# A written-out order of 1,500 steps is replaced by another one, and TensorE's matrix products of zeros are taken out

## The chip, the core and the metric

The kernel runs on one core of a Trainium2 chip. The core has a matrix engine (TensorE, PE in the profile), a vector engine (VectorE, DVE), a scalar engine (ScalarE, ACT), a general engine (GpSimd, POOL) and a sequencer that only issues DMAs (SyncE, SP); PEld is TensorE's loading of weights, which overlaps its products. Each engine takes its own instructions strictly in the order in which the program gives them, and waits on semaphores for the others. Sixteen DMA engines move data for all of them. The metric is the time of the kernel on the device in microseconds (us).

## What is computed

The reference is a linear attention whose output goes through a gated long convolution. B is 8, heads 8, S 576, head size 64, features 128, model width 512.

```python
def phi(x):                                   # q and k, with one w_phi [64, 128]
    proj = x @ w_phi
    proj = proj - max(abs(proj), axis=-1)
    return concat([exp(proj), exp(-proj)])    # 256 features
kv  = k_p^T @ v ;  z = sum(k_p)               # per batch and head
att = (q_p @ kv) / (q_p @ z + 1e-6)
x   = att as [B, S, 512]
x1, x2, x3 = split(x @ w_proj, 3)             # w_proj [512, 1536]
x2c = irfft(rfft(x2) * rfft(filter))          # circular convolution over S = 576
out = (x1 * x2c * x3) @ w_out
```

## The kernel before

All data of a batch stay in SBUF; matrix products are in bf16. The work is cut into small methods of one class, and the whole program is one string, `PLAN`: a list of some 1,500 words, each a method with its arguments and, after `@`, the first of the PSUM banks (eight) that it uses. `run()` (line 958) goes through the string and calls the methods:

```python
for word in PLAN.split():
    name, _, bank = word.partition("@")
    self.bank = int(bank) if bank else None
    f, *args = name.split(",")
    getattr(self, f)(*[int(a) if a.isdigit() else a for a in args])
```

So the string fixes the order of instructions on each engine, the engine of those steps that name one (DVE, ACT or POOL), and the banks. Nothing else sets the order: words of different engines stand in one list, but only words of the same engine are ordered by it, and the framework adds the semaphores for data, buffers and banks. `RING` (line 20) says how many buffers a name has.

What the words are, by stage (b is the batch, v a quarter of its rows, X a half):

- **Loads.** `loadh` (L540, halves, batch 0 only) and `load` (L534) bring q, k or v from HBM and cast them to bf16; POOL issues them. `w_load` brings w_phi (SP, L498) and a third of w_proj or w_out (POOL, L502, L505). `filt_load` (SP, L424) brings the filter in 18 pieces.
- **Transposes.** Batch 0 is transposed on TensorE: `T` (L570) and its eviction `Te`. Later batches go through DMA transposes issued by SP: `trh` (L550) for half of q or k, `trm` (L685) for the maxima of q, `trx` (L770) and `trxt` (L775) for the attention's output, `gen_fwd` (L402) and `gen_fwd5` (L407) once for the Fourier matrices.
- **Features.** `Pk` and `Qn` (L589, L596; `Pkt`, `Qnt` L603 for the last ninth of the rows) project k and q; `maxk`, `maxq` (DVE, L656) take the absolute maximum; `ex`, `exkt`, `exqt` (ACT, L640 to L650) the exponentials. `mhi` and `mlo` split the maxima of q into two bf16 parts, `trm` transposes them, and `Pq`, `Pqt` (L617, L623) project q once more, transposed, with the maxima subtracted inside TensorE. So the first `Pq` of a batch needs `trm` to have landed.
- **Attention.** `em` (ACT) and `vs` (POOL, L696) scale v with the maxima of k, `KV` (L711) makes kv and z, `NE`, `NEt` (L732, L741) the numerator and denominator, `rc`, `xn`, `xnt` (DVE) divide.
- **Gate.** `X1`, `X3` (L846) and `X2` (L803, L807) are the three projections; `fold` and `foldt` build sums and differences of x for `X2`. `F` (L444, L460) is the forward Fourier transform, `m1`, `m2`, `m3` the product with the filter's transform (which `H`, `H_ev` make once from `filt_fold`), `I` the inverse transform, `Ie`, `Ip`, `Im` put its halves together, `tm` multiplies x1 by x3, `ym` the result by the convolution, `O` (L938) is the last projection, with `Oa` and `Ob` as its first three quarters and its last in the last batch, `Oe` its eviction and `st` (SP, L954) the store.
- **Zeros.** `warm,n,k` (L300) issues n matrix products of a tile of zeros, 128 x 128k, whose result nobody reads. There are 20 such words with 58 products.
- **Tables.** `gen_rows` to `gen_sin` build the Fourier matrices by sines on ACT, `gen_sel`, `gen_selx` a selection matrix on POOL. [...]

Of the kernel before, what the change touches and what calls it, by code (L numbers as in the profile page):

```python
# [1010 lines left out]
```

## Time and profile before

| | |
|---|---|
| median of 4 runs | 320.96 us (319.53 to 325.91) |
| the profiled execution | 321.4 us, of which its span is 319.6 |
| busy: PE, DVE, ACT, POOL | 284.8, 247.6, 232.2, 222.6 us |
| mean granted clock of TensorE | 0.96 |
| moved by DMA | 41.52 MB |
| products of zeros (L300) | 58, busy for 13.22 us |

The page gives the busy time of each engine, then the span in 40 slices of 8 us with the busy share of each in tenths, the clock that TensorE was granted (9 is 90% or more), and the mean busy share of the DMA engines. Further views give the busy time by stage, the groups of instructions by line, who waited for whom, the chain of work that ended last, and the instructions of one engine in order of time. A busy share of TensorE is modelled and is not TensorE at its peak.

### The profile page before, as it was taken

The numbers are of one execution on the slowest core, as the hardware profiler recorded it, in microseconds if no ns is written. First come the engines' busy times: TensorE is split into PE (matmuls) and PEld (weight loads), VectorE is DVE, ScalarE is ACT, GpSimd is POOL, SyncE is SP. The second block draws the span as 40 slices with busy tenths as digits, with TensorE's granted clock in tenths as the row PEclk, the third lists the DMA queues.
The fourth block names the chain that finished last, engine by engine and source line by source line (L and its number), as shares of the span: only waits on it lengthen the run. The fifth ranks groups of instructions, "written<-read, shape, count | busy, mean of one in ns | idle before, by whom it ended". The sixth has DMA issues, their size and how long they took to land.

```text
span 319.6 us, 9475 instructions
## 1 busy us (share of the span) xinstructions
PE 284.8 (89%) x3915; PEld 163.9 (51%) x3959; DVE 247.6 (77%) x409; ACT 232.2 (73%) x366; POOL 222.6 (70%) x174
## 2 busy tenths in 40 slices
PE   6666597999868999999999999999999999999981
PEld 2344373565554556555656654664475555654430
DVE  4698589799656997889879887898779777767850
ACT  5697586989647778988788777887787787434531
POOL 8859933779854888779679698847879668813230
PEclk9687589999989999999999999999999999999999
DMA  6999999999999998667994546367953223331416
GB/s 116 238 193 171 180 186 171 141 203 166 166 111 169 178 169 154 135 116 112 148 208 105 131 109 113 19 115 140 160 124 75 63 69 53 75 83 34 98 40 159
DMA packets 78667, 41.52 MB, mean 130 GB/s; under 512 B 58976, under 2 KB 73440, under 8 KB 78624
## 3 DMA queue, kind: packets, MB, share of 16 engines
q1 hardware_dynamic: 63808, 24.66, 42.8%
q0 software_dynamic: 14816, 16.25, 36.2%
q8 instruction: 31, 0.51, 0.7%
q14 instruction: 12, 0.10, 0.1%
HBM read 33.75 MB, written 9.44 MB: 135 GB/s over the span
## 4 chain that ended last, share of the span: by engine, by line
PE 76%; DMA 12%; POOL 4%; DVE 3%; issue 3%; ACT 2%; SPq 0%; POOLq 0%; DVEq 0%; ACTq 0%
PE ps L846 17%; PE ps L938 9%; PE ps L803 8%; PE ps L897 8%; DMA mT<-mh 6%; PE ps L460 6%; PE ps L711 6%; PE ps L732 5%; PE ps L617 2%; PE ps L589 2%; PE ps L623 2%; DMA qn<-in_q_dram 2%; DMA xTt<-xnt 2%; PE ps L596 2%; PE ps L853 2%
## 5 line engine op out<-in xcount | busy, mean ns | idle before, releaser
L846 PE MATMUL ps<-xT,wproj 128*128 128x512 bf16 x244 | 62.8, 380 | 0.5
L915 POOL TENSOR_TENSOR yT<-cv,x1s 128x576 bf16<-128x576 f32 x27 | 34.7, 1290 | 30.6 <-DVE cv L905 18.9
L656 DVE TENSOR_REDUCE mq<-ps 128x8 f32<-128x1024 f32 (+1 forms) x40 | 44.1, 1114 | 14.6 <-PE ps L596 12.0
L656 DVE TENSOR_REDUCE mk<-ps 128x8 f32<-128x1024 f32 (+1 forms) x40 | 44.4, 1113 | 6.5 <-PE ps L589 4.1
L696 POOL TENSOR_TENSOR vm<-vn,vm 128x1152 bf16<-128x1152 bf16 x16 | 34.5, 2154 | 11.8 <-ACT vm L690 9.8
L640 ACT ACTIVATE Eqm<-ps 128x1024 bf16<-128x1024 f32 x32 | 32.9, 1028 | 10.0 <-PE ps L623 6.1
L696 POOL TENSOR_TENSOR vp<-vn,vp 128x1152 bf16<-128x1152 bf16 x16 | 34.4, 2149 | 7.8 <-ACT vp L690 5.8
L834 POOL TENSOR_TENSOR t<-C,B 128x1024 bf16<-128x1024 bf16 x15 | 31.8, 2125 | 10.3 <-ACT C L716 9.3
L938 PE MATMUL ps<-wout,yT 128*128 128x512 bf16 x133 | 34.8, 379 | 1.3 <-DVE yT L915 0.8
L640 ACT ACTIVATE Ekm<-ps 128x1024 bf16<-128x1024 f32 x32 | 32.5, 1028 | 4.7 <-PE ps L589 4.1
L897 PE MATMUL ps<-inv,Y 128*128 128x288 bf16 (+1 forms) x192 | 35.6, 289 | 0.1
L640 ACT ACTIVATE Eqp<-ps 128x1024 bf16<-128x1024 f32 x32 | 32.5, 1023 | 3.9 <-PE ps L623 3.8
L640 ACT ACTIVATE Ekp<-ps 128x1024 bf16<-128x1024 f32 x32 | 32.6, 1030 | 3.7 <-DVE mk L656 2.4
L846 PEld LDWEIGHTS <-wproj 128*128 128x128 bf16 x256 | 23.0, 98 | 23.5 <-issue 0.2
L803 PE MATMUL ps<-wproj,eo 128*128 128x512 bf16 x119 | 30.5, 381 | 1.5 <-issue 1.1
L905 DVE TENSOR_TENSOR cv<-es,ps 128x288 f32<-128x288 f32 x64 | 26.2, 448 | 7.2 <-PE ps L897 4.0
L829 DVE TENSOR_TENSOR Y<-ps,A 128x1024 bf16<-128x1024 f32 (+1 forms) x24 | 24.8, 1044 | 6.9 <-PE ps L460 3.0
L839 POOL TENSOR_TENSOR Y<-Y,t 128x1024 bf16<-128x1024 bf16 x12 | 25.5, 2123 | 5.6 <-DVE Y L839 3.5
L716 ACT COPY o<-ps 128x512 f32<-128x512 f32 x27 | 15.8, 587 | 13.6 <-PE ps L938 10.8
L883 DVE TENSOR_TENSOR x1s<-ps,x1s 128x512 bf16<-128x512 f32 x32 | 21.8, 686 | 4.4 <-PE ps L846 3.9
L716 ACT CAST x1s<-ps 128x512 bf16<-128x512 f32 (+1 forms) x34 | 18.7, 553 | 7.0 <-PE ps L846 4.0
L716 ACT CAST x2n<-ps 128x512 bf16<-128x512 f32 (+1 forms) x32 | 16.2, 520 | 10.3 <-PE ps L803 6.8
(149 smaller groups left out, 636.5 us busy)
## 6 DMA issues: line engine op xcount, KB each, us to landing
out_dram<-o SPq DMA_DIRECT2D x72, 128.0 KB, 2.4
vn<-in_v_dram POOLq DMA_DIRECT2D x8, 576.0 KB, 7.8
kn<-in_k_dram POOLq DMA_DIRECT2D x7, 576.0 KB, 9.0
qn<-in_q_dram POOLq DMA_DIRECT2D x7, 576.0 KB, 8.2
wproj<-in_moe_w_proj_dram POOLq DMA_DIRECT2D x3, 512.0 KB, 8.1
fl<-in_moe_filter_fft_dram SPq DMA_DIRECT2D x18, 64.0 KB, 5.1
kn<-in_k_dram POOLq DMA_DIRECT2D x2, 288.0 KB, 5.5
qn<-in_q_dram POOLq DMA_DIRECT2D x2, 288.0 KB, 8.0
```

What stands on the lines that cost most here:

```text
L640: self.nc.scalar.activation(e, self.db(), AF.Exp, bias=0.0, scale=1.0 if g == "p" else -1.0)
L656: self.nc.vector.tensor_reduce(out=out, in_=src, axis=AX.X, op=ALU.max, apply_absolute_value=True)
L696: self.port(eng, self.elem(eng).tensor_tensor(out=t[:, :, :, 0:64], in0=self.at("vn", b)[:, 2 * X:2 * X + 2], in1=t[:, :, :, 64:65].to_bro ...
L716: self.nc.scalar.copy(dst, src)
L803: self.mm(self.pb(0), eo[:, kt, 128 * c:128 * c + 128], w[:, kt, 512:1024], start=(kt == 0), stop=(kt == 3))
L834: self.port(eng, self.elem(eng).tensor_tensor(out=self.at("t2", b)[:, t, :], in0=self.at("C", b)[:, o, :], in1=self.at("B"), op=ALU.mult))
L839: self.port(eng, self.elem(eng).tensor_tensor(out=Y, in0=Y, in1=self.at("t2", b)[:, i:i + 3:2, :], op=ALU.add if i else ALU.subtract))
L846: self.mm(self.pb(0), w[:, kt, f0 + 128 * m:f0 + 128 * m + 128], x[:, kt, :], start=(kt == 0), stop=(kt == 3))
L897: self.mm(self.pb(0, 0, 288), y, t, start=(k == 0), stop=(k == 2))
L905: self.nc.vector.tensor_tensor(out=self.at("cv", 4 * b + m)[:, :, odd, :], in0=e, in1=o, op=ALU.subtract if odd else ALU.add)
L915: self.port(eng, self.elem(eng).tensor_tensor(out=self.at("yT", b)[:, m, 0:SEQ], in0=self.at("cv", 4 * b + m).rearrange("p j h t -> p (j h ...
L938: self.mm(self.pb(0), y[:, kt, 128 * j:128 * j + 128], w[:, kt, :], start=first and kt == ks[0], stop=last and kt == ks[-1])
```

## The change

Only `PLAN` is different: 156 lines of words become 158. The methods, the tiles, the rings and the number of buffers are the same, and so is each product, eviction and transfer, with three kinds of difference:

- the order of all words, and with it the order on each engine, and the banks;
- the engine of some steps: `gen_turns` 1, some `Te`, four `KVe`, `mlo` of two batches, and some evictions and elementwise steps of `X1e`, `X2e`, `Fe`, `Oe`, `H_ev`, `fold`, `foldt`, `m2`, `m3` and `ym` change between ACT, DVE and POOL;
- the 20 `warm` words are gone.

The beginning and the end of both plans, as the diff has them:

```diff
-zeros loadh,k,0,1 w_load,phi gen_rows gen_cols,0 gen_cols,1 gen_turns,ACT,0 gen_angles,0 loadh,k,0,0
-gen_ident warm,10,4@0 T,k,0,1,0@0 loadh,q,0,0 warm,1,4@1 warm,7,1@1 T,k,0,0,1@1 gen_turns,ACT,1
-gen_angles,1 T,k,0,1,1@2 Te,DVE,k,0,1,1@2 loadh,q,0,1 T,k,0,0,0@3 Te,DVE,k,0,0,0@3 gen_selidx
-gen_pads load,v,0 load,k,1 gen_sin,0 Te,DVE,k,0,0,1@1 w_phi,ACT warm,2,4@4 warm,3,1@4 T,q,0,0,1@4
-Te,DVE,k,0,1,0@0 gen_sin,1 warm,5,4@5 warm,2,1@5 Pk,0,0@2 maxk,0,0@2 warm,1,4@1 warm,3,1@1 Pkt,0@0
-ex,k,p,0,0@2 maxkt,0@0 exkt,m,0@0 Pk,0,1@6 gen_sel gen_selx Te,ACT,q,0,0,1@4 load,q,1 maxk,0,1@6
-em,p,0,0 T,q,0,0,0@5 exkt,p,0@0 Te,DVE,q,0,0,0@5 warm,2,4@4 warm,1,1@4 Qn,0,1@4 ex,k,m,0,0@2
-gen_five maxq,0,1@4 Pk,0,3@0 maxk,0,3@0 em,m,0,0 vs,POOL,m,0,0 T,q,0,1,1@2 Te,DVE,q,0,1,1@2
-T,q,0,1,0@3 ex,k,m,0,1@6 Te,ACT,q,0,1,0@3 vs,POOL,p,0,0 ex,k,p,0,1@6 ex,k,p,0,3@0 ex,k,m,0,3@0
-Qn,0,0@4 maxq,0,0@4 Pk,0,2@2 maxk,0,2@2 em,m,0,1 Qn,0,2@6 maxq,0,2@6 Qnt,0@4 maxqt,0@4 w_load,proj,1
-ex,k,p,0,2@2 ex,k,m,0,2@2 em,p,0,1 Qn,0,3@0 maxq,0,3@0 mhi,0 vs,POOL,m,0,1 mlo,POOL,0 filt_load,SP,0
-filt_load,SP,1 filt_fold,POOL,2 KV,0,0@6 load,k,2 trh,k,1,0 Pk,1,0@4 trh,k,1,1 Pk,1,1@2 maxk,1,0@4
-ex,k,m,1,1@2 trh,q,1,1 warm,2,4@0 Qn,1,2@0 ex,k,m,1,0@4 KVe,DVE,0,0@6 trh,q,1,0 maxk,1,1@2
-ex,k,p,1,0@4 Qn,1,3@6 ex,k,p,1,1@2 maxq,1,3@6 maxq,1,2@0 vs,POOL,p,0,1 trm,0 Pq,0,0@4 ex,q,m,0,0@4
-load,v,1 Qn,1,1@6 maxq,1,1@6 ex,q,p,0,0@4 Pq,0,1@2 filt_fold,POOL,1 ex,q,m,0,1@2 Qnt,1@0 maxqt,1@0
-ex,q,p,0,1@2 Qn,1,0@4 maxq,1,0@4 w_load,proj,0 NE,0,0@6 rc,0,0@6 xn,0,0@6 Pq,0,3@0 ex,q,m,0,3@0
-ex,q,p,0,3@0 filt_fold,POOL,0 Pkt,1@2 maxkt,1@2 em,m,1,0 KV,0,1@4 KVe,DVE,0,1@4 NE,0,1@6 mhi,1
-rc,0,1@6 exkt,m,1@2 mlo,POOL,1 vs,POOL,m,1,0 load,q,2 xn,0,1@6 gen_fwd5 Pqt,0@0 exqt,p,0@0
-exkt,p,1@2 NE,0,3@4 rc,0,3@4 xn,0,3@4 exqt,m,0@0 Pk,1,3@6 maxk,1,3@6 Pq,0,2@4 ex,q,m,0,2@4 H,4@2
-NEt,0@0 H_ev,DVE,4@2 rct,0@0 xnt,0,1@0 ex,q,p,0,2@4 xnt,0,0@0 gen_fwd ex,k,p,1,3@6 ex,k,m,1,3@6
-warm,2,4@3 Pk,1,2@2 maxk,1,2@2 NE,0,2@4 rc,0,2@4 xn,0,2@4 ex,k,m,1,2@2 H,1@0 H_ev,DVE,3@0 em,p,1,0
-ex,k,p,1,2@2 H_ev,DVE,1@0 trx,0,0 H,0@6 H_ev,DVE,2@6 H_ev,DVE,0@6 trh,k,2,0 vs,POOL,p,1,0 gen_inv
-trm,1 Pq,1,1@4 ex,q,m,1,1@4 H_fix late load,q,3 trx,0,3 trx,0,1 ex,q,p,1,1@4 Pq,1,0@0 ex,q,p,1,0@0
-warm,3,4@2 warm,2,1@2 KV,1,0@2 KVe,ACT,1,0@2 Pk,2,1@6 trx,0,2 X1,0,1@4 ex,q,m,1,0@0 fold,DVE,0,0
...
-load,k,3 em,p,2,0 Qn,2,1@0 m2,POOL,0,1 Pq,1,3@2 ex,q,p,1,3@2 m3,POOL,0,1 m2,POOL,0,0 maxq,2,1@0
-Qnt,2@4 maxqt,2@4 ex,q,m,1,3@2 F,0,4@6 m1,0,4@6 Pq,1,2@0 ex,q,p,1,2@0 Qn,2,2@4 maxq,2,2@4 X1,0,3@7
-X1e,ACT,0,3@7 m3,POOL,0,0 ex,q,m,1,2@0 Qn,2,0@2 maxq,2,0@2 mhi,2 X1,0,2@6 trx,1,1 X1e,ACT,0,2@6
-mlo,POOL,2 Pk,2,3@4 maxk,2,3@4 em,m,2,0 X3,0,1@7 tm,0,1@7 Pk,2,2@0 ex,k,m,2,2@0 load,q,4 NE,1,3@2
-rc,1,3@2 xn,1,3@2 trx,1,0 trh,q,3,0 vs,POOL,p,2,0 vs,POOL,m,2,0 X3t,0@6 tmt,0@6 X3,0,0@7 tm,0,0@7
-ex,k,m,2,3@4 ex,k,p,2,2@0 NE,1,2@2 rc,1,2@2 trh,q,3,1 xn,1,2@2 ex,k,p,2,3@4 I,0,1,0@6 Ie,0,1@6
-maxk,2,2@0 X3,0,3@7 I,0,0,0@2 Ie,0,0@2 em,p,2,1 em,m,2,1 load,k,4 vs,POOL,m,2,1 tm,0,3@7 I,0,0,1@3
-NEt,1@4 trm,2 Pq,2,0@0 ex,q,p,2,0@0 ex,q,m,2,0@0 rct,1@4 xnt,1,1@4 xnt,1,0@4 Pq,2,1@6 ex,q,p,2,1@6
-I,0,1,1@2 Ip,0,1@2 Im,0,1@2 X3,0,2@4 vs,POOL,p,2,1 Ip,0,0@3 I,0,2,0@5 trx,1,3 Im,0,0@3 warm,3,1@2
-Qn,3,0@0 maxq,3,0@0 Ie,0,2@5 trx,1,2 warm,3,1@2 KV,2,0@2 tm,0,2@4 w_load,out ex,q,m,2,1@6 Qn,3,3@0
-maxq,3,3@0 KVe,ACT,2,0@2 trh,k,3,0 fold,DVE,1,0 I,0,3,0@5 Ie,0,3@5 Pq,2,2@6 ex,q,m,2,2@6 NE,2,0@2
...
-tmt,6@7 foldt,POOL,7,1 O,5,4@7 Oe,ACT,5,4@7 I,6,3,0@4 X2,7,4@1 I,6,2,1@7 X2e,ACT,7,4@1 X2e,ACT,7,5@1
-X1t,7@0 tm,6,3@3 tm,6,0@5 I,6,2,0@5 Im,6,0@6 Ip,6,0@6 Ie,6,2@5 I,6,3,1@1 ym,POOL,6,1 Ie,6,3@4
-trx,7,0 fold,DVE,7,0 Ip,6,3@1 X1,7,2@6 X2,7,1@3 X2,7,0@4 X2e,ACT,7,0@4 st,5,0 X2e,ACT,7,1@3
-fold,DVE,7,1 X2,7,2@5 X2e,ACT,7,2@5 st,5,4 Oe,DVE,5,3@2 X2,7,3@2 X2e,ACT,7,3@2 Im,6,3@1 ym,DVE,6,0
-Ip,6,2@7 Im,6,2@7 ym,POOL,6,2 ym,DVE,6,3 X3t,7@1 X1te,DVE,7@0 X1,7,1@3 X1e,ACT,7,1@3 F,7,0@4
-Fe,ACT,7,0@4 m2,POOL,7,1 tmt,7@1 F,7,1@2 O,6,0@7 Oe,ACT,6,0@7 m1,7,0@4 O,6,1@1 X1,7,0@0 m1,7,1@2
-m3,DVE,7,1 F,7,4@7 m1,7,4@7 O,6,2@4 st,5,3 Oe,ACT,6,1@1 st,6,0 X3,7,1@1 Fe,ACT,7,1@2 X3,7,0@7
-Oe,ACT,6,2@4 m2,DVE,7,0 m3,DVE,7,0 I,7,0,0@4 st,6,1 st,6,2 X1e,ACT,7,0@0 tm,7,0@7 I,7,0,1@0 Ie,7,0@4
-Ip,7,0@0 Im,7,0@0 ym,POOL,7,0 I,7,1,0@5 Ie,7,1@5 X1e,ACT,7,2@6 I,7,1,1@2 Im,7,1@2 Ip,7,1@2 O,6,3@4
-Oe,ACT,6,3@4 I,7,2,0@0 tm,7,1@1 I,7,2,1@5 Ie,7,2@0 Ip,7,2@5 Im,7,2@5 st,6,3 I,7,3,0@3 Ie,7,3@3
-I,7,3,1@4 X3,7,2@2 tm,7,2@2 ym,POOL,7,1 Im,7,3@4 X1,7,3@3 ym,POOL,7,2 X1e,ACT,7,3@3 X3,7,3@5
-Ip,7,3@4 tm,7,3@5 ym,DVE,7,3 Oa,7,0@4 Ob,7,0@4 Oe,ACT,7,0@4 Ob,7,1@5 st,7,0 Oa,7,1@5 Oe,ACT,7,1@5
-st,7,1 Oa,7,2@4 Ob,7,2@4 Oe,ACT,7,2@4 st,7,2 Ob,7,3@5 Oa,7,3@5 Oe,ACT,7,3@5 st,7,3 yt,DVE,7 Oa,7,4@4
-Ob,7,4@4 Oe,ACT,7,4@4 st,7,4
+w_load,phi zeros w_phi,ACT loadh,k,0,1 gen_rows gen_cols,0 gen_turns,ACT,0 loadh,k,0,0 gen_cols,1
+gen_turns,DVE,1 gen_angles,1 gen_sin,1 gen_angles,0 gen_ident T,k,0,0,0@0 Te,ACT,k,0,0,0@0
+T,k,0,0,1@1 Te,ACT,k,0,0,1@1 T,k,0,1,0@2 Te,DVE,k,0,1,0@2 loadh,q,0,0 T,q,0,0,1@3 Te,DVE,q,0,0,1@3
+loadh,q,0,1 gen_pads gen_sin,0 T,k,0,1,1@4 Pk,0,0@0 maxk,0,0@0 ex,k,m,0,0@0 ex,k,p,0,0@0
+Te,DVE,k,0,1,1@4 T,q,0,0,0@5 Te,DVE,q,0,0,0@5 Pkt,0@2 load,v,0 gen_selidx maxkt,0@2 exkt,p,0@2
+filt_load,SP,1 Pk,0,1@6 maxk,0,1@6 Qn,0,1@4 maxq,0,1@4 load,k,1 T,q,0,1,0@0 Te,DVE,q,0,1,0@0
+exkt,m,0@2 Qn,0,0@4 maxq,0,0@4 em,p,0,0 gen_sel T,q,0,1,1@1 Pk,0,3@2 maxk,0,3@2 load,q,1
+ex,k,m,0,1@6 filt_load,SP,0 em,m,0,0 Te,ACT,q,0,1,1@1 Qnt,0@0 maxqt,0@0 ex,k,p,0,1@6 Pk,0,2@4
+ex,k,p,0,2@4 ex,k,m,0,2@4 trh,k,1,0 Qn,0,3@6 maxq,0,3@6 gen_selx trh,q,1,1 ex,k,m,0,3@2 ex,k,p,0,3@2
+maxk,0,2@4 em,p,0,1 Qn,0,2@0 maxq,0,2@0 em,m,0,1 Pk,1,0@6 trh,q,1,0 w_load,proj,1 vs,POOL,p,0,0
+vs,POOL,m,0,0 KV,0,0@4 gen_five mhi,0 mlo,DVE,0 trm,0 Qn,1,3@0 KVe,DVE,0,0@4 ex,k,m,1,0@6
+ex,k,p,1,0@6 Pk,1,1@2 ex,k,m,1,1@2 ex,k,p,1,1@2 maxq,1,3@0 maxk,1,0@6 maxk,1,1@2 Qn,1,2@4 maxq,1,2@4
+Pq,0,0@0 ex,q,m,0,0@0 Qn,1,1@6 ex,q,p,0,0@0 Pq,0,1@2 ex,q,p,0,1@2 ex,q,m,0,1@2 gen_fwd trh,k,1,1
+Pq,0,3@0 gen_fwd5 load,k,2 trh,k,2,1 trh,k,2,0 maxq,1,1@6 NE,0,0@4 ex,q,p,0,3@0 rc,0,0@4 xn,0,0@4
+Pkt,1@6 maxkt,1@6 trx,0,0 load,v,1 ex,q,m,0,3@0 NE,0,1@2 rc,0,1@2 xn,0,1@2 trx,0,1 vs,POOL,p,0,1
+vs,POOL,m,0,1 KV,0,1@4 KVe,DVE,0,1@4 exkt,m,1@6 exkt,p,1@6 em,m,1,0 Qn,1,0@0 maxq,1,0@0 Pq,0,2@2
+ex,q,m,0,2@2 NE,0,3@4 ex,q,p,0,2@2 rc,0,3@4 xn,0,3@4 Pk,1,2@6 Qnt,1@0 em,p,1,0 w_load,proj,0
+maxqt,1@0 mhi,1 filt_fold,POOL,0 Pqt,0@4 exqt,p,0@4 maxk,1,2@6 Pk,1,3@2 trx,0,3 filt_fold,POOL,2
+load,q,2 NE,0,2@0 rc,0,2@0 xn,0,2@0 exqt,m,0@4 NEt,0@4 filt_fold,POOL,1 maxk,1,3@2 vs,POOL,m,1,0
+H,1@0 ex,k,m,1,2@6 ex,k,p,1,2@6 mlo,POOL,1 trm,1 rct,0@4 xnt,0,0@4 em,m,1,1 xnt,0,1@4 H_ev,DVE,3@0
+vs,POOL,p,1,0 gen_inv ex,k,m,1,3@2 H,0@6 H_ev,ACT,1@0 H_ev,DVE,0@6 ex,k,p,1,3@2 KV,1,0@4
+KVe,DVE,1,0@4 trx,0,2 fold,POOL,0,1 H_fix H_ev,DVE,2@6 trxt,0 load,q,3 trh,q,2,0 Pq,1,0@0
+ex,q,p,1,0@0 ex,q,m,1,0@0 Pq,1,1@2 ex,q,m,1,1@2 ex,q,p,1,1@2 w_load,proj,2 Pk,2,0@4 maxk,2,0@4
+foldt,DVE,0,0 H,4@0 H_ev,DVE,4@0 ex,k,m,2,0@4 NE,1,0@6 rc,1,0@6 xn,1,0@6 X1,0,1@1 X1e,DVE,0,1@1
+em,p,1,1 X1,0,0@2 X2,0,3@3 ex,k,p,2,0@4 Pk,2,1@6 ex,k,p,2,1@6 Qn,2,1@0 ex,k,m,2,1@6 foldt,POOL,0,1
+late X2e,DVE,0,3@3 maxq,2,1@0 X2,0,4@4 X2e,DVE,0,4@4 X2,0,2@3 X2e,ACT,0,2@3 maxk,2,1@6 fold,POOL,0,0
+X2,0,0@5 X2e,ACT,0,5@4 vs,POOL,p,1,1 X2,0,1@0 X1e,ACT,0,0@2 X2e,ACT,0,1@0 X2e,DVE,0,0@5 Qn,2,0@6
+maxq,2,0@6 Pqt,1@2 exqt,p,1@2 exqt,m,1@2 trh,q,2,1 Qnt,2@4 maxqt,2@4 F,0,0@0 trh,q,3,0 Fe,ACT,0,0@0
...
+X1te,ACT,0@3 maxk,2,2@0 F,0,4@6 m1,0,4@6 Pk,2,3@2 maxk,2,3@2 m3,POOL,0,0 ex,q,p,1,2@4 ex,k,m,2,2@0
+X1,0,3@7 X1e,ACT,0,3@7 mlo,POOL,2 X3t,0@4 tmt,0@4 X3,0,3@6 tm,0,3@6 NE,1,2@0 rc,1,2@0 m3,POOL,0,1
+I,0,0,0@7 vs,POOL,p,2,0 em,m,2,0 vs,POOL,m,2,0 em,p,2,1 vs,POOL,p,2,1 trm,2 ex,k,p,2,3@2 xn,1,2@0
+trx,1,1 ex,k,m,2,3@2 NE,1,3@4 rc,1,3@4 trh,k,3,0 xn,1,3@4 X3,0,2@6 Qn,3,3@0 maxq,3,3@0 Ie,0,0@7
+Pq,2,1@2 ex,q,m,2,1@2 ex,q,p,2,1@2 Qnt,3@4 maxqt,3@4 X3,0,1@7 em,m,2,1 Qn,3,0@0 maxq,3,0@0 Pq,2,0@4
+ex,q,m,2,0@4 ex,q,p,2,0@4 NEt,1@2 trx,1,2 KV,2,0@0 KVe,ACT,2,0@0 rct,1@2 xnt,1,0@2 xnt,1,1@2 trx,1,3
+tm,0,1@7 I,0,0,1@2 Ip,0,0@2 Im,0,0@2 I,0,1,0@3 Ie,0,1@3 tm,0,2@6 Pq,2,2@4 ex,q,p,2,2@4 NE,2,0@0
+rc,2,0@0 ex,q,m,2,2@4 xn,2,0@0 vs,POOL,m,2,1 KV,2,1@2 KVe,ACT,2,1@2 trh,k,3,1 fold,DVE,1,1 Pq,2,3@6
+ex,q,p,2,3@6 Qn,3,2@0 maxq,3,2@0 trxt,1 ex,q,m,2,3@6 trx,2,0 load,q,4 NE,2,1@4 rc,2,1@4 xn,2,1@4
+trx,2,1 X2,1,2@2 X2e,ACT,1,2@2 w_load,out load,k,4 X2,1,3@3 X2e,DVE,1,3@3 I,0,2,0@0 Ie,0,2@0
+fold,POOL,1,0 Qn,3,1@6 ym,POOL,0,0 maxq,3,1@6 Pk,3,0@4 ex,k,m,3,0@4 I,0,1,1@1 Ip,0,1@1 Im,0,1@1
+X2,1,1@3 X2e,ACT,1,1@3 I,0,3,0@0 I,0,2,1@2 Im,0,2@2 NE,2,3@6 ex,k,p,3,0@4 Ie,0,3@0 X2,1,0@3
...
+trx,7,3 X2,7,4@5 X2e,ACT,7,4@5 I,6,3,1@7 Ip,6,0@6 Ie,6,2@2 I,6,3,0@6 tm,6,2@4 I,6,2,1@0 O,5,3@4
+X1,7,1@2 Im,6,1@3 Ie,6,3@6 fold,DVE,7,0 X2,7,0@6 X2e,ACT,7,0@6 fold,DVE,7,1 st,5,0 Oe,ACT,5,3@4
+X2,7,3@3 X2,7,1@1 X2e,ACT,7,1@1 ym,DVE,6,1 Im,6,3@7 X2e,DVE,7,3@3 X2,7,2@4 X2e,ACT,7,2@4 X3,7,1@3
+ym,POOL,6,0 Im,6,2@0 Ip,6,2@0 X1e,ACT,7,1@2 ym,POOL,6,2 X2e,DVE,7,5@5 F,7,0@4 Fe,ACT,7,0@4 F,7,1@0
+Ip,6,3@7 ym,DVE,6,3 O,6,0@2 tm,7,1@3 m1,7,1@0 m2,POOL,7,1 st,5,2 Oe,ACT,6,0@2 st,5,4 st,6,0 m1,7,0@4
+m3,DVE,7,1 X1t,7@3 X1te,ACT,7@3 Fe,ACT,7,1@0 m2,DVE,7,0 m3,DVE,7,0 F,7,4@7 m1,7,4@7 X1,7,2@6 O,6,2@4
+st,5,3 X3t,7@5 X1e,ACT,7,2@6 X1,7,0@6 X3,7,0@0 X1e,ACT,7,0@6 tm,7,0@0 tmt,7@5 I,7,0,0@7 I,7,0,1@6
+Ie,7,0@7 Ip,7,0@6 Oe,ACT,6,2@4 st,6,2 I,7,1,0@1 Ie,7,1@1 Im,7,0@6 ym,POOL,7,0 I,7,1,1@3 O,6,3@2
+Oe,ACT,6,3@2 X3,7,2@7 I,7,2,0@6 Ie,7,2@6 I,7,2,1@2 I,7,3,0@1 Im,7,1@3 Ip,7,1@3 Ie,7,3@1 tm,7,2@7
+Im,7,2@2 I,7,3,1@3 Ip,7,2@2 ym,POOL,7,1 st,6,3 Ip,7,3@3 Im,7,3@3 X1,7,3@0 X3,7,3@1 O,6,1@2
+X1e,ACT,7,3@0 tm,7,3@1 Oe,ACT,6,1@2 ym,POOL,7,2 Oa,7,0@3 ym,DVE,7,3 Ob,7,0@3 Ob,7,2@2 st,6,1
+Oe,ACT,7,0@3 st,7,0 Ob,7,1@1 Oa,7,1@1 Oe,ACT,7,1@1 st,7,1 Ob,7,3@3 Oa,7,2@2 Oe,ACT,7,2@2 st,7,2
+Oa,7,3@3 Oe,ACT,7,3@3 st,7,3 yt,DVE,7 Oa,7,4@1 Ob,7,4@1 Oe,ACT,7,4@1 st,7,4
```

In the left-out lines the words are the same in kind, in another order.

## The prediction

> **What bounds the kernel now.** I read the page first, for where TensorE stops being full; then the busy time by stage; then the chain in order of time; then POOL's own instructions, because the chain leads to a transfer.
>
> ```profile
> span 319.6 us, 9475 instructions
> PE 284.8 (89%) x3915; PEld 163.9 (51%) x3959; DVE 247.6 (77%) x409; ACT 232.2 (73%) x366; POOL 222.6 (70%) x174
> PE   6666597999868999999999999999999999999981
> PEclk9687589999989999999999999999999999999999
> DMA  6999999999999998667994546367953223331416
> ```
>
> TensorE is nearly full from the thirteenth slice on, and the DMA engines are full over just those slices in which it is not. By stages:
>
> ```profile
> 16.00:27.00 11.00, 7.14 (x141) 5.40 (x142) 10.96 (x16) 10.07 (x16) 7.07 (x5) 0.81 1.26 207
> 27.00:36.00 9.00, 3.69 (x74) 2.59 (x70) 5.46 (x6) 4.01 (x6) 8.69 (x9) 0.69 1.16 140
> 36.00:57.00 21.00, 17.30 (x345) 11.98 (x342) 17.93 (x34) 16.72 (x23) 10.31 (x10) 0.86 1.17 185
> 57.00:91.00 34.00, 31.34 (x508) 18.76 (x512) 28.57 (x42) 28.68 (x46) 26.90 (x19) 1.00 1.32 169
> 100.00:290.00 190.00, 186.08 (x2553) 106.10 (x2588) 156.38 (x251) 145.43 (x236) 142.93 (x97) 1.00 0.65 115
> ```
>
> After the span the columns are the busy time of PE, weight loads, DVE, ACT and POOL, then granted clock, DMA share and GB/s. From 100 to 290 us PE is idle for 3.9 us: no order can win more than that there. From 16 to 27 us DVE is the full one; from 27 to 36 us nobody but the DMA engines is. The chain says for whom:
>
> ```profile
> 25.17 2.16 POOL vm L696
> 27.76 7.54 DMA mT<-mh
> 35.34 0.62 PE ps L623 x8
> 47.19 6.37 DMA mT<-mh
> 53.60 0.40 PE ps L623 x8
> 54.44 0.86 PE ps L300 x5
> 76.90 6.54 DMA mT<-mh
> 83.48 0.40 PE ps L623 x8
> ```
>
> Three times a small transpose (the maxima of q, step trm) holds the first Pq of a batch, for 6.4 to 7.5 us, though the eight trm take 3.0 us in the median. What stands before it comes from POOL:
>
> ```profile
> 15.38 0.85 POOL L534 DMA_DIRECT2D qn<-in_q_dram  x1
> 20.14 2.14 POOL L696 TENSOR_TENSOR vm<-vn,vm 128x1152 bf16<-128x1152 bf16 x1 [3.90 <-ACT vm L690]
> 24.34 0.81 POOL L502 DMA_DIRECT2D wproj<-in_moe_w_proj_dram  x1
> 30.22 0.81 POOL L534 DMA_DIRECT2D kn<-in_k_dram  x1
> ```
>
> Adding each DMA's time to landing to its issue gives, in order of issue whatever queue it came from: trh k,1,0 at 25.1, trh k,1,1 at 26.0, trh q,1,1 at 30.7, w_load proj,1 at 32.4, trh q,1,0 at 35.1, trm,0 at 35.3, load k,2 at 39.0, load v,1 at 42.7. SP's transposes and POOL's loads land in one line. A load that POOL issues early is a load that a later transpose stands behind.
>
> **The change part by part.** The sum is made on the profiled execution, 321.4 us (span 319.6 and 1.8 around it), which is 0.4 above the median of the four runs, 320.96. Matrix products other than those of zeros, transfers and evictions are the same in number; only some evictions and elementwise steps change engine (Fe, KVe, X2e, fold and others, each 0.6 to 1.2 us on DVE or ACT, 2.1 for a fold on POOL).
>
> *The first 16 us.* Before, the zeros of warm,5,4 stand between the last transposed block (12.0) and Pk,0,0 (14.56); ACT then begins its first exponential at 16.47. After, Pk,0,0 waits only for T,q,0,0,1, which needs the q half that lands at 11.95 (unmoved: the POOL steps before it are the same), and ACT for gen_sin 0 and the table load of 1.28: some 14.2. So the first exponential is about 2 us earlier, an estimate from these rows. gen_turns 1 goes from ACT (1.65) to DVE, beside waits. What hides the gain is late next: the transfers.
>
> *POOL's loads.* In the new order w_load proj,1 comes ahead of both vs of batch 0, directly behind gen_selx. POOL is free of gen_sel, the q load (0.85) and gen_selx (2.10) by 15.2, so it is issued at 15.2, not 24.34. The vs (2.14 each) wait for em, at 17.3 to 19; behind them follow load k,2 and load v,1 at once, at 21.6 to 24 instead of 30.22 and 33.20.
>
> *SP's order.* It becomes trh k,1,0, trh q,1,1, trh q,1,0, trm,0; trh k,1,1 and both gen_fwd go behind trm,0. The first still waits for the k load (9.60 + 10.8 = 20.4), and three transposes are issued at 1.3 to 2.3 us each, the q ones after the q load lands, about 24: trm,0 is issued at 25.5 to 27 (27.76 before).
>
> *When trm,0 lands.* From 20.4 to 35.3 before, the line served the q load (2.75, the step between the landings of v and k before it), four transposes (1.0 each, 25.1 to 26.0), w_load (4.6, between the landings of v,1 and w_load proj,0), trm (0.2): 11.5 of 14.9 us; 3.4 went between. After, one transpose is gone (-1.0); the loads k,2 and v,1 stand ahead (+2.75 each). Neither ahead gives 34.3; both give 39.8. POOL reaches them 2 to 4 us before SP reaches trm,0, so both are ahead; the loads lie closer together, and I give back half of the 3.4: 38.0. In the same way trh k,1,0 lands behind w_load, at 27 to 29 instead of 25.1, and in TensorE's order Pk,1,0 and behind it KV,0,0 (25.47 before) wait for that; Pkt,1, and behind it NE,0,1 and KV,0,1, wait for trh k,1,1.
>
> *To the first X1.* From the first Pq's exponentials to NE,1,0, ACT has in the new order 14 exponentials (0.93 each from start to start), five small ones and the casts, and one H_ev (1.2): 16.8 us; with the 4.3 us that ACT is idle in the stage from 36 to 57 us it makes 38.0 + 16.8 + 4 = 58.8 against 56.7. PE has then 0.5 us more of its work done. This costs +1.6.
>
> *trm,2.* Load q,4 is issued at 76.20, just ahead of trm,2 at 76.90, and both land at 83.4. After, load q,4 stands behind trx,2,0. PE waits 1.4 us there and Pq,2,0 to Pq,2,1 takes 1.55 more than its work; I take -1.5.
>
> *The zeros.* All 58 go. Those of the first 46 us lie in waits; their effect on the clock is the second rival. After 56 us they are busy for 0.85 + 0.68 us (56 to 70, 70 to 100), with TensorE otherwise full: -1.2.
>
> *The tail.* X1,7,3 ends its loads of weights at 306.27; X1e, tm and ym follow, and Ob,7,0 starts at 309.28. Between lie X3,7,3 and Oa (1.5 us), and PE stands for 1.1. After, O,6,1 (0.86) lies there too: -0.9. The stores behind it keep their spacing of 1.29.
>
> *The rest, 100 to 290 us.* TensorE's distance from NE to X, F to I, and Qn to Pq is counted over in both plans and is alike within 3 us of work, and all above what the trace needs. I take 0, with +2 and -2 as ends: 3.9 us of idle time is the most that can go, and an equal amount is what I allow to come.
>
> Sum: 1.6 - 1.5 - 1.2 - 0.9 = -2.0, so 319.4 on the profiled execution and 319.0 on the median.
>
> [...] The rows show a granted clock of 0.81 and 0.69 in the stages before 36 us with the zeros in.
>
> **The rivals.**
>
> *The loads cost more (the other side).* Place: trm,0. If the line moves no faster than before, it lands at 39.8, and if the loads and transposes slow each other as at gen_fwd (13.7 us to landing among two loads), at 42 or later. Every us goes into the first X1. At 40 the whole gain is gone; from 41.6 on the kernel is over 0.5% slower; 42 gives 323.0, 44 gives 325.0. For it: POOL waits for nothing that holds w_load back. Against it: the loads done early are missing from the line before trm,1.
>
> *The clock.* Without zeros TensorE keeps half clock until it has enough work, perhaps through the first X1 and X2. The shortest stretch of half clock in the trace, from 93.1 to 96.5 us, is 3.4 long; one or two such, under full work, cost 1.7 to 3.4: 320.7 to 322.4. Against it: from 36 to 57 us PE is busy for 17.3 of 21 us.
>
> *The transposes slip through.* trm,0 lands at 32 to 34; the first Pq, DVE and ACT follow, and the gain of the first 16 us is kept: 314.5 to 316.5. For it: there is one transpose less ahead. Against it: the line.
>
> *Nothing moves.* Work per stage is alike in both plans, and the waits only change place: 321.
>
> **How the numbers follow.** Forecast 0.37, with its own range 317 to 321; the loads 0.34; the clock 0.10; slip through 0.14; nothing 0.05. 0.5% is 1.6 us, about what a measurement of this kernel can tell from no change. Faster (below 319.4): two thirds of the forecast's case and the third rival, 0.40. Same: the rest of the forecast's, most of the clock's, and nothing moving, 0.22. Slower: the loads and what is left, 0.38. 315 cuts off the better part of the third rival, 325 the last of the first.
>
> **What would show it.** Right: w_load proj,1 issued at 15 to 16 and k,2 before 25; trh k,1,0 landing after 27, trm,0 at 37 to 39; the first X1 at 58 to 60; no wait of PE for mT in batch 2; PE idle under 0.5 us before Ob,7,0. Wrong: trm,0 at 35 or sooner, a granted clock of 0.5 after 57 us, or more than 5 us of idle PE between 100 and 290 us.

## The result and the profile after

The new order takes 0.9927 of the time of the old one, with a 95% interval of 0.9907 to 0.9948: 0.7% less, some 2.3 us of 321. In part of the executions the whole program runs some per cent longer (up to 334.35 us with the new order, 330.39 with the old), with the new order more often than with the old, so that the plain medians over all, 323.25 us against 322.48, show no gain, and the ratio compares only the undisturbed ones. The profiled execution of the new order took 320.55 us against 321.4 before, so its trace shows 0.85 us of the gain. Single traces of this kernel differ by 2 to 3 us; what follows leans on places and waits that recur, and on ratios.

The page of the new kernel, the same rows as before:

```profile
span 318.8 us, 9367 instructions
PE 276.3 (87%) x3857; PEld 162.0 (51%) x3901; DVE 250.7 (79%) x415; ACT 230.3 (72%) x363; POOL 220.5 (69%) x171
PE   0753478899999999998699999999999999999991
PEclk9999999999999999999999999999999999999998
DMA  6999994899889995999968939555439310360346
```

TensorE has less to do in the first slices and is not full until the ninth. A hole is new at the nineteenth and twentieth slice. The granted clock stays at 90% or more until the last slice. By stages (span, busy time of PE, weight loads, DVE, ACT and POOL, granted clock, DMA share, GB/s):

```profile
16.00:27.00 11.00, 4.28 (x53) 2.97 (x53) 9.98 (x14) 8.83 (x16) 8.38 (x7) 1.00 1.23 207
27.00:36.00 9.00, 3.62 (x100) 3.46 (x102) 1.08 (x2) 1.94 (x2) 8.91 (x7) 1.00 1.23 209
36.00:57.00 21.00, 16.51 (x315) 11.91 (x312) 16.75 (x28) 16.49 (x24) 8.28 (x7) 1.00 0.91 156
57.00:91.00 34.00, 31.86 (x562) 19.38 (x561) 32.15 (x49) 29.63 (x45) 31.69 (x22) 1.00 0.98 141
91.00:100.00 9.00, 8.89 (x163) 5.65 (x157) 7.92 (x14) 7.83 (x13) 6.60 (x8) 1.00 1.20 174
100.00:290.00 190.00, 183.62 (x2508) 104.67 (x2537) 155.23 (x252) 143.28 (x232) 137.78 (x92) 1.00 0.73 117
```

From 27 to 36 us DVE and ACT have nearly stopped (1.08 and 1.94 us, against 5.46 and 4.01). From 91 to 100 us TensorE is full, where before it was busy for 6.71 of 9 us. From 100 to 290 us it is idle for 6.4 us, against 3.9.

To see where time goes, count TensorE's steps in order, each with its duration free of waits and the zeros left out, and ask when the same amount of work has been begun. Against before (negative is ahead; the first column is the moment in before's trace; the other kernels are told of below). The values are estimates: with other durations for the steps single ones shift by up to 1 us.

```
before at, us    after   loads late   mix_a   mix_b   mix_c
   25.5           +2.2     -1.5        +0.1    +0.2    +0.2
   63.5           +4.2     +1.6        +1.8    -0.8    +3.3
   84.5           +2.1      0.0        +0.2    -2.3    +2.2
   90.1           +1.6      0.0        +0.2    -2.7    +1.8
  103.5           -3.8     -4.9        -3.1    -6.0    -1.5
  122.8           -3.9     -3.8        -3.1    -6.0    -1.5
  144.9           -3.4     -1.3        -2.7    -5.5    -1.1
  155.9           +0.2     -1.3        -2.9    -0.7    -1.2
  end             -0.9     -0.9        -4.1    -1.5    -2.5
```

So the new front loses 4.2 us by 63 us. It wins 2.6 back by 90 us and 5.4 more by 103 us, gives 3.6 back between 145 and 156 us, and gains 0.9 in the tail.

**The front.** The chain in order of time (start, us, what) says what the first X1, now at 61.1, waits for:

```profile
35.37 8.92 DMA kT<-kn
...
44.34 0.29 PE ps L601 x2
44.63 0.99 PE ps L730 x16
45.62 2.10 PE ps L709 x72
```

It is not the small transpose mT (landed at 38.09) but trh k,1,1, which the new order puts behind trm,0 and gen_fwd. It is issued at 35.37 and lands at 44.3; Pkt,1 (L601) waits for it, and behind Pkt,1 come NE,0,1 and KV,0,1 (L709). How much of the 4.2 us belongs to the order is less sure: four later kernels have before's words up to this point (loads late, mix_a, mix_b, mix_c), and in their traces the first X1 comes at 58.3, 58.3, 56.2 and 60.3 us, against 56.7 in before.

**91 to 95 us in before.** The largest single gain comes from a wait that the prediction didn't speak of. Before's stages there, its chain, and its transfers from 90.2 to 91.7 us:

```profile
91.00:100.00 9.00, 6.71 (x127) 4.67 (x128) 4.91 (x7) 4.92 (x7) 5.55 (x6) 0.81 1.27 110
93.10:96.50 3.40, 3.25 (x87) 2.72 (x82) 0.59 (x1) 1.51 (x3) 2.01 (x2) 0.50 1.52 83
```

```profile
90.17 0.33 PE ps L596 x8
90.50 0.03 PE ps L711 x2
90.53 2.41 issue
92.94 2.02 PE ps L711 x70
```

```profile
q1 hardware_dynamic: 640, 0.16, 192.2%
q8 instruction: 1, 0.02, 5.3%
```

TensorE stops in the middle of KV,2,1, after the first products, with nothing that the profile shows to wait for ("issue"), and its next 70 products run at half rate (2.02 us; the 72 of KV,2,0 take 1.26; granted clock 0.50). The queue row points to the cause: one 16 KB packet of instructions, on the DMA engines from 90.3 to 91.6 us. The last section counts this out. In the new order that packet lands at 89.5, 2.2 us before it is needed.

**145 to 156 us in after.** The lead is given back at two steps: 1.0 us in KV,4,0, at the end of another block of instructions (the next one's packet lands at 150.0), and 2.0 us ahead of X2,3,0, which waits for a fold and so for the transpose trx,3,1:

```profile
148.08 0.18 SPq L768
148.26 0.05 issue
148.31 6.90 DMA xT<-xn
```

trx,3,3 had held SP from 143.5 to 148.3 before trx,3,1 could be issued.

### The profile page after: what moved, and what is told of

It reads as the page before. It is cut to its first block, busy times and chain, and to the rows that moved or that the text cites. A ratio compares the mean times of both kernels' runs of the same rounds, so it can differ in the third digit from the quotient of the medians.

```text
span 318.8 us, 9367 instructions
## 1 busy us (share of the span) xinstructions
PE 276.3 (87%) x3857; PEld 162.0 (51%) x3901; DVE 250.7 (79%) x415; ACT 230.3 (72%) x363; POOL 220.5 (69%) x171
## 4 chain that ended last, share of the span: by engine, by line
PE 72%; DVE 11%; DMA 6%; issue 3%; POOL 3%; ACT 2%; SPq 1%; DVEq 0%; POOLq 0%; ACTq 0%
PE ps L844 16%; PE ps L801 9%; PE ps L895 8%; PE ps L936 8%; PE ps L458 5%; PE ps L730 5%; PE ps L709 5%; DMA kT<-kn 3%; DVE mq L654 3%; PE ps L851 2%; DMA xT<-xn 2%; PE ps L587 2%; PE ps L594 2%; PE ps L615 2%; PE ps L621 2%
## 5 line engine op out<-in xcount | busy, mean ns | idle before, releaser
L913 POOL TENSOR_TENSOR yT<-cv,x1s 128x576 bf16<-128x576 f32 x27 | 34.3, 1279 | 31.1 <-DVE cv L903 14.0
L832 POOL TENSOR_TENSOR t<-C,B 128x1024 bf16<-128x1024 bf16 x13 | 27.5, 2120 | 12.5 <-ACT C L714 9.5
L837 POOL TENSOR_TENSOR Y<-Y,t 128x1024 bf16<-128x1024 bf16 x14 | 29.6, 2124 | 2.3 <-DVE Y L827 1.1
L714 ACT COPY o<-ps 128x512 f32<-128x512 f32 x29 | 17.0, 591 | 12.4 <-PE ps L936 6.5
L714 ACT CAST x1s<-ps 128x512 bf16<-128x512 f32 (+1 forms) x30 | 16.6, 552 | 11.4 <-PE ps L844 9.6
L785 POOL TENSOR_TENSOR eo<-xT 128x1024 bf16<-128x1024 bf16 x8 | 17.0, 2130 | 10.5 <-DVE eo L785 5.3
```

The lines of the kernel that those rows point to most:

```text
L714: self.nc.scalar.copy(dst, src)
L832: self.port(eng, self.elem(eng).tensor_tensor(out=self.at("t2", b)[:, t, :], in0=self.at("C", b)[:, o, :], in1=self.at("B"), op=ALU.mult))
L837: self.port(eng, self.elem(eng).tensor_tensor(out=Y, in0=Y, in1=self.at("t2", b)[:, i:i + 3:2, :], op=ALU.add if i else ALU.subtract))
L913: self.port(eng, self.elem(eng).tensor_tensor(out=self.at("yT", b)[:, m, 0:SEQ], in0=self.at("cv", 4 * b + m).rearrange("p j h t -> p (j h ...
```

## The experiments

None of these kernels leaves out a step of the computation; the zeros feed nothing. Ratios are to the kernel before, unless another is named.

**The zeros.** Three kernels: before without all 58, before without the 46 ahead of the first X1, and after with 57 put back into its waits.

```
before_no_zeros:        - all 20 words warm,...
before_no_early_zeros:  - the 15 words warm,... ahead of X1,0,0
after_with_zeros:       + warm,16,4 ahead of T,k,0,0,0   + warm,4,4 ahead of T,q,0,0,1 and Qn,0,0
                        + warm,14,4 ahead of Pk,1,0 and of Qn,1,3   + warm,5,4 ahead of Qn,1,1
```

> The kernel before with the 58 products of zeros left out and nothing else changed. Theory Z (the zeros alone are the gain): 0.993 to 0.996 of before, 1.2 to 2.3 us. Theory O (the order is the gain, the zeros of the first 46 us lie in waits): only those behind 56 us count, 0.85 + 0.68 us, 0.995 to 0.999. Theory C (without them TensorE's products take twice as long in the front and the first X1 comes later): 1.000 to 1.007, the first X1 at 57.5 to 59 instead of 56.7.

> The kernel before without the 46 products of zeros ahead of the first X1; the 12 behind it stay. Theory C (the early zeros earn their place: without them TensorE's products take twice as long in the front, each release of DVE and ACT comes later, and the time rises, as it did by 0.8% with all 58 gone): 1.003 to 1.010 of before, blocks at 107 ns instead of 56 before 17 us and Pq's products at 54 instead of 28 up to 45 us. Theory O (they lie in waits): 0.997 to 1.002, and the 0.8% came from elsewhere.

> The kernel after with 57 products of zeros put into the waits that TensorE has there before 38 us, and no others. Theory C (the half rate of the first 47 us costs time): the transposed blocks take 56 ns instead of 107, Pq's products 28 instead of 54, and the first X1 comes 1 to 3 us before 61.1; time 0.993 to 0.998 of after. Theory O: the front is set by landings, the products get faster and the first X1 stays within 0.6 us of 61.1; time within 0.4% of after, or up to 1 us slower where zeros stand in the way of a landed transpose.

Measured: without all of them 1.0083 (1.0036 to 1.0131); without the early ones 0.9998 (0.9959 to 1.0037); after with zeros 1.0053 (0.998 to 1.0125), beside 0.9948 for after in the same comparison.

Without the early zeros TensorE does run at half rate: the transposed blocks follow each other at 107 ns instead of 56. The time stays the same, the first X1 comes at 57.1 instead of 56.7, and theory C falls. Zeros put into after's waits don't help, and seem to cost time (the two intervals overlap): the 14 ahead of Pk,1,0 still run when its transpose has landed (29.1), and Pk,1,0 starts at 31.1, 2.0 us later. That trace tests theory C only in part, since the transposed blocks stay at half rate in it and the products reach the full one at 23 us. The loss of all 58, taken with the early run, points to the last 12. But their own worth on TensorE is small: from 60 to 78 us an order without them gains 0.2 us on the same with them, and from 84 to 90 us 0.4. Why leaving them out makes the kernel slower isn't settled; mix_b comes back to it.

**One transpose back in the front.**

```
 trh,k,1,0
+trh,k,1,1
 ... trh,q,1,1 ... trh,q,1,0 ... trm,0 ... gen_fwd
-trh,k,1,1
```

> The kernel after with the second transpose of k of batch 1 (trh k,1,1) put back directly behind the first, ahead of those of q, where before has it. Theory K (the first X1 at 61.1 is late because Pkt,1 and KV,0,1 wait for trh k,1,1, which lands at 44.3 behind trm,0 and gen_fwd): it lands before 31, KV,0,1 starts at 41 to 43 instead of 45.55, the first X1 at 57.5 to 60, and what stands behind it by 90 us is 1 to 3 us earlier; time 0.992 to 0.998 of after. Theory M (trm,0 alone sets it): trm,0 lands 1 to 3 us later than 38.1, the first X1 at 62 to 64; time 1.000 to 1.008 of after.

Measured: 1.0038 (0.9982 to 1.0093), some 1% more than after. Theory K falls as a cure. Beside the next trace (328.25 us, this one 328.1), trh k,1,1 is issued 17 us earlier (22.1 against 39.1), but trm,0 is issued 4.9 us later (37.1) and mT lands 5.2 us later (47.1); the first X1 moves by 0.9 us only. I read it so that the front is short of transfers, and not of a better order among these few; that wasn't tested further.

**After once more.**

```
(no change)
```

> The kernel after, unchanged, for a second execution's trace. If the loss of 3.6 us of TensorE at 150 to 156 us (trx,3,1 landing after 6.9 us, behind transfers that took 12 to 20) belongs to the order, this trace has it within 2 us of the same place and size. If it belongs to a stretch of some us in which the DMA engines move 27 to 70 GB/s and which falls anywhere, the trace has none there, KV,5,1 starts at 199 to 201 instead of 203.6, and the profiled execution is 2 to 3.5 us shorter. Time 0.991 to 0.995 of before.

Measured: 0.9948 (0.990 to 0.9995). Its profiled execution took 328.25 us. It gives back as much, 2.1 us of it in a stop of TensorE one block of instructions earlier than in the first. All traces with after's order behind 90 us together say more. Counted as in the table, from 134 to 165 us of before, four of them lose 3.6 to 4.6 us (both of after, the one with trh k,1,1 first, mix_b), and three lose under 1 us (after with zeros, and two told of below: before's order up to KV,2,1, and mix_a). So the loss comes back with this order, but the order behind 90 us doesn't decide it alone.

**The halves.** All steps up to KV,2,1 and its eviction (some 90 us) in one order, the rest in the other.

```
hyb_after_front:   words of after up to KVe,2,1  + words of before that are left
hyb_before_front:  words of before up to KVe,2,1 + words of after that are left
```

> The order of after up to KV,2,1 and its eviction (some 90 us), and from there all that is left in the order of before. Theory F (the gain lies in the front: the transposes of batches 2 and 3 are issued there ahead of load q,4 and load k,4, so neither Pq,2 nor Pk,3,0 waits as in before at 81.7 and 91 to 94.7 us): 0.990 to 0.996 of before, and Pk,3,0 waits under 1 us. Theory R (the gain lies in the order from 90 us on): the front is 1.6 us late at 90 us, and the kernel takes 1.000 to 1.007 of before.

> The order of before, with its zeros, up to KV,2,1 and its eviction, and from there all that is left in the order of after. Theory F: load q,4, load k,4 and trh k,3,0 stand as in before, so the waits at 81.7 and 91 us stay; only the tail's 0.9 us can be won: 0.996 to 1.001 of before. Theory R: 0.990 to 0.996.

Measured: 1.0072 (1.0013 to 1.0131) and 1.0006 (0.9953 to 1.0059). Neither half holds the gain: after's front costs time with before's rest behind it, and after's rest wins nothing behind before's front, which still holds load q,4 and load k,4 early. In that one TensorE still stops in KV,2,1, for 4.2 us.

**The two loads alone (loads late in the table).**

```
-load,q,4  (behind mlo,2)     -load,k,4  (behind em,m,2,1)
+load,q,4  (ahead of w_load,out)     +load,k,4  (behind w_load,out)
```

> The kernel before with two loads of POOL moved, load q,4 and load k,4, to directly before and behind w_load,out, where after has them. Theory F: trm,2 and trh k,3,0 no longer stand behind them in the line; mT lands within 4.5 us of its issue instead of 6.5, trh k,3,0 within 6 instead of 11, Pq,2,1 starts 1 us earlier and Pk,3,0 2 to 4 us earlier; time 0.988 to 0.996 of before. Rival (the wait moves on): trh k,4,0 stands on SP until load k,4 has landed, some 96 us instead of 93.4, and trm,3 and Pk,4,0 behind it come late; what is won at 90 us is gone by 125; 0.998 to 1.004.

Measured: 0.9995 (0.9943 to 1.0046). The waits go, as theory F has it: Pq,2,1 follows Pq,2,0 at once, and TensorE doesn't stop in KV,2,1 (the packet lands at 87.2, 3.1 us before it is needed). At 103 us the kernel is 4.9 us ahead. The rival is right about the time: of that, 3.6 are gone at 134 us. The place was another than it named. The chain leads to a store:

```profile
115.12 0.54 SPq L954
115.66 0.05 issue
115.71 7.09 DMA out_dram<-o
```

The store takes 7.1 us to land where it took 3.9 before, since it now stands behind load v,4, issued 1.5 us ahead of it; the eviction Oe,0,3 waits for its buffer, and I,1,3,1 of TensorE for that eviction's bank.

**The tail alone (before_tail).**

```
-O,6,1@1 (ahead of X1,7,0)  -Oe,ACT,6,1@1  -st,6,1
 X3,7,3@5
+O,6,1@2
 tm,7,3@5
+Oe,ACT,6,1@2 ... +st,6,1 (behind Ob,7,0)
```

> The kernel before with one step of the tail moved as in after: O,6,1 (0.86 us of TensorE), its eviction and its stores come behind X3,7,3 and not before X1,7,0. If the idle time before Ob,7,0 (1.4 us) is filled by it: X3,7,3 starts 0.86 us earlier, the idle time falls to 0.3 to 0.6, and the time by 0.6 to 1.0 us, 0.997 to 0.998. If the path through X1,7,3 and ym is what ends last and O,6,1 delays it: no change, 0.999 to 1.002.

Measured: 0.9969 (0.9921 to 1.0018), which contains both the expected 0.997 and no change. The trace decides for the place: from the start of KV,7,1 to that of Ob,7,0 it is 37.89 us against 38.73, 0.84 less, and TensorE's wait ahead of Ob,7,0 falls from 1.13 to 0.63 us.

**Before's front, without the two loads, and after's rest.**

```
mix_a:  words of before up to KVe,2,1, without load,q,4 and load,k,4  + words of after that are left
mix_b:  mix_a without its 12 late products of zeros
mix_c:  mix_b, with  -load,q,6 (behind maxq,4,2)  +load,q,6 (behind load,k,6)
```

> The order of before, with its zeros, up to KV,2,1 and its eviction, but without load q,4 and load k,4, which come with the rest; the rest in the order of after. Theory J (the gain needs both: batch 2 and 3's transposes ahead of the two loads, and an order behind 90 us that does not give it back as before's does at 121 to 133): the waits before Pq,2,1 and Pk,3,0 fall below 0.5 us, TensorE is 3 to 5 us ahead of before at 103 us and still 2 to 5 ahead at the end; 0.985 to 0.993 of before, since the front of before is also 1.6 us earlier at 90 us than that of after. Rival (what is won at 90 us is lost again in any order, because TensorE catches up with the transfers): under 1.5 us ahead at the end; 0.996 to 1.003.

> The kernel of mix_a without the 12 products of zeros behind the first X1 (63 to 87 us in the profile of before: 0.85 + 0.68 us busy). Theory Z (late zeros cost what they are busy): 1.0 to 1.5 us less than mix_a, 0.995 to 0.997 of it. Rival (they lie beside waits or keep TensorE at full rate): within 0.5 us of mix_a.

> The kernel of mix_b with one load moved: load q,6 (issued at 129.4 us there, first read at 175.5) comes behind load k,6 (148.1). Theory L (the lead of 5.5 us that mix_b has at 143 us is given back at 143 to 156 us because trx,3,3 and trx,3,1 stand behind trh k,5,0 and load q,6 in the line of transfers): trx,3,1 is issued at 143 to 145 instead of 147.1, the waits before O,1,3 and X2,3,0 (2.97 and 2.00 us) fall below 0.7 together, and the end comes 3 to 5 us before that of mix_b: 0.980 to 0.988 of before. Rival (the stretch from 128 to 150 us is slow by itself, with few bytes moved whatever stands in the line): the waits stay over 3 us together or come back behind trh q,6,0 at 175, and the time is 0.996 to 1.004 of before, as mix_b's 1.0015.

Measured: mix_a 0.9882 (0.9844 to 0.9920), mix_b 1.0015 (0.9968 to 1.0061), mix_c 0.9889 (0.9831 to 0.9947). mix_a is theory J to the letter, and with mix_c the fastest of the kernels that were run: no wait before Pq,2,1, no stop in KV,2,1, 3.1 us ahead at 103 us and 4.1 at the end. It differs from the kernel with before's order up to KV,2,1 (1.0006) in the place of load q,4 and load k,4 alone, so with after's rest behind it that place is worth 1.2%, where with before's rest it was worth nothing (0.9995). The three by stages, first mix_a:

```profile
136.00:144.00 8.00, 7.89 (x122) 4.93 (x123) 6.69 (x11) 6.97 (x13) 7.80 (x4) 1.00 1.31 136
144.00:156.00 12.00, 11.89 (x170) 7.00 (x169) 10.57 (x19) 9.32 (x19) 9.87 (x8) 1.00 1.20 153
```

mix_b:

```profile
136.00:144.00 8.00, 7.76 (x132) 5.24 (x128) 6.96 (x13) 6.97 (x14) 7.92 (x5) 1.00 1.35 87
144.00:156.00 12.00, 6.84 (x110) 3.97 (x112) 5.56 (x9) 6.25 (x13) 4.42 (x5) 1.00 1.25 145
```

mix_c:

```profile
136.00:144.00 8.00, 7.95 (x105) 4.39 (x104) 6.74 (x10) 6.53 (x13) 6.20 (x3) 1.00 1.35 107
144.00:156.00 12.00, 11.84 (x183) 7.29 (x185) 11.02 (x20) 9.93 (x20) 10.89 (x9) 1.00 0.74 122
```

mix_b is 5.5 us ahead when it comes to 143 us, and TensorE is then busy for 6.84 of 12 us: it gives 4.8 of the 5.5 back, 2.95 at the end of the same block of instructions as after and 2.0 ahead of X2,3,0. The first of these ends with a late packet of instructions (the last section), where theory L saw a transpose. The line of transfers is behind there: trx,3,3 holds SP from 141.4 to 147.0, and trx,3,1 lands at 154.3. With load q,6 out of that line (nothing reads it before 175 us) trx,3,1 lands 3.8 us after its issue instead of 7.2, and the time falls by 1.3% against mix_b. That is theory L in the ratio; in the one trace of mix_c the front came 4 us later than in that of mix_b, so the lead that would have been lost wasn't there to lose. Load q,6 isn't enough by itself either: mix_a has it in the same place as mix_b, and there trx,3,1 lands 5.6 us after its issue and nothing is lost. What the 12 zeros of mix_a do stays open: they are worth 0.6 us of TensorE at most and their absence cost 1.3%, but mix_c runs as fast as mix_a without them.

## Why the prediction was right, and where it was wrong

The forecast was 319.0, 0.6% less than before; measured is 0.7% less. The number is right in good part by luck: the sum has two wrong sizes and two missing terms that nearly cancel.

- **Two readings of the lines.** The 6.4 to 7.5 us of the three small transposes are times from issue to landing; TensorE stood for 3.5, 2.4 and 1.4 us of them. And from 27 to 36 us POOL is full beside the DMA engines (8.69 of 9 us).
- **The first 16 us: half.** Pk,0,0 came 2.06 us earlier as said, the first exponential only 1.03 (15.44). ACT waits for gen_sin 0, and that for DVE, which got gen_turns 1 on top (its last angle ends at 12.67). That cover, "beside waits", wasn't there. Nothing of the gain reached the first X1.
- **POOL's loads: right.** k,2 and v,1 were issued at 22.80 and 23.60 (21.6 to 24 was said). w_load proj,1 came at 17.36, not at 15.2: gen_sel started at 12.84, right behind DVE's last angle (12.67), because the kernel's `port` makes a marked step of POOL wait for the last marked step of DVE.
- **When trm,0 lands: right by two errors.** 38.09 against 38.0, and trh k,1,0 at 27.63. But trm,0 was issued at 31.97 instead of 25.5 to 27: with the loads ahead, trh q,1,1 and trh q,1,0 took 3.3 and 4.8 us to issue, where the sum had 1.3 to 2.3. The time in the line was that much shorter.
- **The line in order of issue: right.** The twelve loads and transposes issued from 20 to 42 us land in the order of their issue across both queues, but for one pair (w_load proj,0 and trm,0, 0.6 us apart). trm,0, issued at 32.0 us with four of them not yet landed, took 6.1 us to land; trm,1, at 52.1 us with one, took 2.3.
- **To the first X1: wrong, 61.1 instead of 58.8** (in TensorE's work +4.2 instead of +1.6). The step "38.0 + 16.8 + 4" went along the first Pq. The path went along trh k,1,1, which the prediction named ("Pkt,1, and behind it NE,0,1 and KV,0,1, wait for trh k,1,1") and didn't price: it lands at 44.3.
- **trm,2 and the zeros: about right together.** mT lands 3.0 us after its issue instead of 6.5, and 2.6 us came back from 63 to 90 us; -1.5 and -1.2 had been said. The split was off: by the pairs with and without them, the late zeros give 0.6.
- **91 to 100 us: missing.** This stage was left out of the table that the prediction shows. It held the largest term, -5.4: 2.4 us for the stop in KV,2,1, an estimated 1.7 for the half rate (half of the 3.4 us from 93.1 to 96.5), and some 1.1 for a second stop of the same kind at 99.9.
- **100 to 290 us: outside its bound.** "0, with +2 and -2": it was +3.6 in the profiled execution, and TensorE's idle time of 6.4 us is over the 5 that had been named as a sign of error. The plans were compared by TensorE's distances, and not by what stands in the line of transfers from 128 to 150 us.
- **The tail: right.** -0.9, and before_tail has 0.84 of it alone. TensorE's wait ahead of Ob,7,0 is 0.63 in after, not under 0.5.

Sum of the profiled execution: +4.2 at 63 us, -2.6, -5.4, +3.6 with small changes around it, -0.9 in the tail, -0.9 in all.

Of the rivals, the first was right that the front costs more, but not about the place: trm,0 came at 38.1, and later stages paid the 4.2 us back. The clock as a rival was wrong twice: the half rate came, until about 49 us (up to 48.7 us a product of the small transposes took 311 ns, against 216 in before from 43 us on), and cost nothing that the runs show (0.9998 without the early zeros); and the shortest half-rate stretch, which had been priced as a risk of the change, was one of the things that it removed. In before the granted clock fell to 0.50, from 93.1 to 96.5 us, after a stop of 2.41 us.

## What to carry to other kernels

Issue a load that is read late behind the transfers that are read soon, on whichever queue they stand: where transfers landed in order of issue, moving two loads by 8 and 11 us took out a wait of 1.5 us and a stop of 2.4, and moving a third brought 1.3%. Such a gain is only a lead: follow it to the next stretch where the DMA engines are full and ask whether their line is ahead there too, since two kernels gave back 3.6 us within 31 us and 4.8 within 13, and the two loads moved alone left the time as it was (0.9995). And price every stage that isn't full, the short ones too, and every wait that the prediction itself names.

## What was not expected of the hardware

**Packets of instructions come on the same DMA engines, and where one lands late TensorE stops.** The pages show 31 instruction packets of q8 with 0.51 MB in before (16 KB each) and 30 in after. That is one for each 255 of TensorE's instructions in before and for each 260 in after, with each weight load and each product counted as one (7918 and 7802), so I read them as TensorE's own. The counts here are twice the number of weight loads (3959 and 3901), since some records of products are missing (3915 and 3857). TensorE stops in before at number 2238. Without all the zeros it stops at 2238 too, and without the early ones as well, though other products stand there. Further such stops, from the start of one instruction to that of the next, are at 704 (before_no_early_zeros, 1.3 us), 1726 (after_with_zeros, 2.0), 2494 (before, 1.3), 3518 (the second execution of after, 2.1), 3774 (after 1.0, mix_b 2.95) and 6076 (before_no_zeros, 1.5): all of these lie 188 to 192 beyond a multiple of 256 (256 of them are called a block here), and each ends 1.2 to 1.6 us after a packet has landed. In before the block that holds KV,2,0 is used up in 4.0 us (86.3 to 90.3), and the packet isn't on the engines until 90.3. In before and in the two kernels that are before without zeros (load q,4 and load k,4 early in all three) the packet lands 1.0 to 1.3 us late; in after, loads late and mix_a it lands 2.2 to 3.1 us ahead. That the packet is late because of the transfers ahead of it is read from this, and not shown in the packet's own queue.

**The granted clock doesn't show the half rate from the start.** After's products of the small transposes (L621) from 36 to 50 us, and the same products of before (L623) from 43 to 57 us:

```profile
L621 PE MATMUL ps<-mT,sel x32: 263/311/311, 38.1 to 48.7; 64*128 64x128 bf16 x32
```

```profile
L623 PE MATMUL ps<-mT,sel x24: 213/216/226, 45.2 to 54.2; 64*128 64x128 bf16 x24
```

The median is 311 against 216 ns, and start to start 54 against 28, while the granted clock of after reads 1.00 throughout. In before, which reads 1.00 from 42 to 93.1 us, the granted clock does show the half rate (0.50 from 93.1 to 96.5 us).

**Stretches in which the line nearly stands.** From 135 to 143 us in after the transfers moved 66 GB/s with a DMA share of 1.37, while four transfers that were issued from 128 to 132 us took 13 to 20 us to land. Before at 94 us (51 GB/s, share 1.75) and mix_b at 137 us (58 GB/s, share 2.10) have the like. No run here tells what slows them.
